# A newly searched order of operations, with sixteen small operations on another engine, in a fused attention and MLP block on one core

## The chip, the cores and the metric

The kernel runs on one NeuronCore of one Trainium2 chip. The metric is the device time of one execution in microseconds (us), taken as the median of several runs. An engine is named as the profile names it: PE is the matmul engine (PEld its weight loads), DVE the vector engine, ACT the scalar engine, POOL the GpSimd engine, and SP the engine whose queue issues all DMA transfers of this kernel.

## What is computed

One transformer-like block on a sequence of 2048 rows of 448 numbers in bf16: a sliding, dilated attention of 16 heads over 8 earlier positions, then a mixer and an MLP, each behind a layer norm.

```python
def _A_ref(x, wqkv, wo):                      # H = 16, W = 8, dilation 2
    q, k, v = split(x @ wqkv)                 # x: (1, 2048, 448)
    logits = einsum(q, k at positions s - 2*w) * scale     # w = 0..7, masked below 0
    return (softmax(logits) @ v at the same positions) @ wo

def _B_ref(x, w1, w2, w3, w4):
    h = gelu(layernorm(x) @ w1)               # 448 -> 448
    hs = (the four quarters of h moved by +1, -1, +2, -2 rows) @ w2
    x1 = x + hs
    return x1 + gelu(layernorm(x1) @ w3) @ w4 # 448 -> 1792 -> 448

h = x + _A_ref(layernorm(x), A_wqkv, A_wo)
out = h + _B_ref(layernorm(h), B_w1, B_w2, B_w3, B_w4)
```

## The kernel before, in words

The sequence is cut into four stretches of 512 rows (t = 0 to 3) for the attention and the mixer, and into five units of 2, 4, 4, 4 and 2 row tiles of 128 (u = 0 to 4) for the MLP. The phase functions only write down operations, each with an engine, its instructions and what it reads and writes; the tag of an operation is the phase and the number of the stretch or unit, so "B20" is phase B2 of unit 0.

- N1 (line 680): statistics of the rows on DVE, the reciprocal root as an Ln and an Exp on ACT, and the normalisation, mostly on DVE.
- A1 (line 696): the transposed rows times the query and key weights; a half of the stretches are transposed by a DMA (`dma_turn`, line 425, "DMA_TRANSPOSE actT<-lntm" in the profile). V (line 743): the values, evicted to vt and moved to vw by DMAs.
- A2 (line 764): four large products of queries and shifted keys on DVE (tile qk_r, 128x4096), each summed over the head by matmuls on PE (ps<-qk_r,zc); then the softmax under the tag S on DVE and ACT.
- A3 (line 814): four products of the attention with a mask on DVE (tile bd_r), the matmuls with vw, and under the tag O the output matmul with wo and the residual.
- B1 (line 860): layer norm and, under the tag M, the matmul with w1 and the gelu on ACT.
- B2 (line 915): the matmul with w2, the sum with the residual on DVE, and under the tag T the layer norm and its transposing DMA; for unit 0 the statistics are sums of squares on ACT. W3 (line 962): the matmul with w3 and the gelu on ACT. B3 (line 979): the matmul with w4, the last sum on DVE and the store.

Operations are numbered from 0 to 872 as they are written down, and the numbers are the same in both kernels. `arrange` (line 197) takes the list ORDER: it goes through it, gives every operation its place in the queue of its engine, and hands out the buffers (8 PSUM banks, 2 of qk_r, 3 of bd_r and so on), first freed first used. Every engine then works through its own queue in that order and waits at each operation on the semaphores of what it needs. An operation that waits holds up all behind it in its queue. OTHER lists the operations that run on their second engine: evictions and normalisations written for ACT then run on DVE, and the additions `xb + xin` of line 957 written for POOL run on DVE. All instructions are issued by one line, so the profile shows nearly every instruction as L1048; a load of ACT's function table shows as L1043 where `emit_engine` sets it ahead of an Exp or Ln that follows a gelu:

```python
            for op in order[e]:
                if op.table == "exp" and table != "exp":
                    eng.preload_act_table_set("natural_log_exp_and_others")
                table = op.table or table
                for (sem, val) in plan_[op.idx]:
                    eng.wait_ge(sem, val)
```

The operations that are spoken of below by number:

- 103: the eviction of the second transposed tile at the start (A10). 196, 198: two normalisations of B10. 510, 513: two evictions of A33.
- 488, 490, 492, 494: the four DVE products of A23 (the queries and keys of stretch 3); 489, 491, 493, 495: the matmuls that sum them (8, 8, 8 and 4 instructions). 497, 501, 502: DVE and PE of its softmax.
- 555: the second pair of matmuls of B20. 557, 556: B20's two residual sums on DVE; 558: minus the mean (nm, DVE); 559, 560: the sums of squares (ACT); 561, 562: Ln and Exp (ACT); 563: nmr (DVE); 564, 565: the two normalisations of T0; 568: the transposing DMA of T0; 577: the first matmul of W30; 579: the first eviction of W30 in the new order (gelu). 310: an Ln of B11.
- 605, 606, 613, 614: the four groups of matmuls of B21, 8 instructions each. 597: the first matmul of B30.
- 300, 308, 309, 313 to 316: last aggregate, Ln, Exp and the four normalisations of B11; 317: its transposing DMA. 481: an eviction of V3.
- 37, 38: the loads of w3, 896 KB each; 486, 487: the loads of w4, 784 KB each; 483, 484, 485: the moves of V3's values to vw (256, 320 and 48 KB).
- 566, 567, 627, 629, 698 to 701, 769 to 771, 830: additions `xb + xin` of the units T0 to T4.

Of the kernel before, what the change touches and what calls it, by code (L numbers as in the profile page):

```python
# [21 lines left out]
STAGE = '....'  # L22
ALONE = False
ORDER = """
# [30 lines left out]
"""  # L55
OTHER = """
103 196 198 510 513 564 565 627 629 699 700 701 769 830
"""
FULL = (4,)
FILL = (1, 1, 0, 0)  # L60
# [1029 lines left out]
```

## Time and profile before

| | us |
|---|---|
| median of 3 runs | 189.72 (188.6, 189.72, 190.02) |
| span of the profiled execution, first to last instruction | 187.0 |
| its own time beside the span | not recorded; the median is 2.7 above the span |
| ACT busy | 124.0 (66% of the span) |
| POOL busy | 20.9 (11%) |
| ACT_TABLE_LOAD | 12 of 1.28 each |
| granted TensorE clock, mean | 1.000 |

The times of the runs hold what lies around the span, so a difference worked out in the span is added to the median. The trace gives each instruction's start and duration; matmuls overlap, so the interval from one start to the next tells what one costs.

### The profile page before, as it was taken

The page shows a single profiled execution, that of the slowest core. Times are in us where ns is not written, and L with a number is a line of the kernel's source. Part 1 is how long each engine was busy: PE and PEld are TensorE (multiplying, and loading weights), DVE is VectorE, ACT ScalarE, POOL GpSimd, SP SyncE. Part 2 cuts the span into 40 slices and gives each one's busy share as a digit, 9 for nine tenths or more (in the row PEclk, how much of TensorE's full clock was granted, in tenths as well). Part 3 has the DMA queues.
Part 4 walks back from the last instruction along what each step waited for, and adds up shares of the span by engine and source line. Part 5 has one row for each costly group of instructions (what it writes and reads, how often), then busy time and mean ns, then how long its engine had stood idle before and what let it go on. Part 6 is the DMA issues. An engine that isn't in the chain of part 4 may idle for free.

```text
span 187.0 us, 5742 instructions
## 1 busy us (share of the span) xinstructions
PE 180.0 (96%) x2482; PEld 93.5 (50%) x2482; DVE 130.8 (70%) x236; ACT 124.0 (66%) x280; POOL 20.9 (11%) x56
## 2 busy tenths in 40 slices
PE   5999999989999989999999999999999999999994
PEld 2685443345453445467455444555444544555663
DVE  7989999999999999999997960089962080000512
ACT  4459989879999999998991987930267004930340
POOL 3440000000003000500042000020034050000000
PEclk9999999999999999999999999999999999999999
DMA  5923583661654697597409060043305031000022
GB/s 151 340 101 58 125 173 63 141 149 17 115 124 94 160 206 301 100 316 146 101 4 140 2 137 4 0 31 84 100 4 112 4 71 60 4 0 0 4 98 74
DMA packets 38609, 18.29 MB, mean 98 GB/s; under 512 B 27464, under 2 KB 38072, under 8 KB 38584
## 3 DMA queue, kind: packets, MB, share of 16 engines
q1 hardware_dynamic: 38584, 17.93, 41.4%
q8 instruction: 19, 0.31, 0.7%
q14 instruction: 6, 0.05, 0.1%
HBM read 8.14 MB, written 1.84 MB: 53 GB/s over the span
## 4 chain that ended last, share of the span: by engine, by line
PE 75%; DVE 16%; ACT 6%; issue 1%; POOL 0%; POOLq 0%
PE ps L1048 75%; DVE bd_r L1048 6%; DVE qk_r L1048 4%; DVE lntm L1048 2%; ACT lntm L1048 1%; DVE xin L1048 1%; DVE st L1048 1%; ACT arena L1048 1%; DVE mx L1048 1%; ACT h3T L1048 1%; ACT L1048 1%; ACT L1043 1%; DVE arena L1048 1%; ACT xin L1048 1%; DVE pb L1048 0%
## 5 line engine op out<-in xcount | busy, mean ns | idle before, releaser
L1048 PE MATMUL ps<-actT,arena 64*128 64x512 bf16 (+2 forms) x812 | 69.6, 326 | 0.3
L1048 ACT ACTIVATE h3T<-ps 128x512 bf16<-128x512 f32 (+1 forms) x70 | 30.7, 520 | 39.1 <-PE ps L1048 38.7
L1048 PEld LDWEIGHTS ps<-actT,arena 64*128 64x128 bf16 (+1 forms) x812 | 35.7, 96 | 29.8 <-PE ps L1048 1.6
L1048 PE MATMUL ps<-arena,h3T 64*128 64x448 bf16 (+3 forms) x434 | 44.5, 343 | 0.0
L1048 DVE SCALAR_TENSOR_TENSOR ost<-ps,mrs,arena 128x448 bf16<-128x448 f32 (+2 forms) x17 | 10.7, 649 | 35.5 <-PE ps L1048 26.9
L1048 ACT ACTIVATE arena<-ps 128x512 bf16<-128x512 f32 (+4 forms) x62 | 31.5, 568 | 2.6 <-PE ps L1048 2.4
L1048 DVE TENSOR_TENSOR qk_r<-arena 128x4096 bf16<-128x4096 bf16 (+1 forms) x16 | 32.1, 2015 | 0.3 <-PE ps L1048 0.3
L1048 PEld LDWEIGHTS ps<-arena,h3T 64*128 64x128 bf16 (+1 forms) x434 | 22.4, 94 | 19.6 <-ACT h3T L1048 0.3
L1048 DVE TENSOR_TENSOR bd_r<-arena,bmask 80x2048 bf16<-80x2048 bf16 x16 | 18.9, 1211 | 0.3 <-ACT arena L1048 0.3
L1048 DVE TENSOR_SCALAR lntm<-arena,mv,rs_y 128x512 bf16<-128x512 f32 x14 | 6.8, 540 | 13.1 <-ACT rs_y L1048 11.6
L1048 POOL TENSOR_TENSOR arena<-arena,xin 128x448 f32<-128x448 f32 x9 | 10.6, 1193 | 34.3 <-DVE lntm L1048 34.3
L1048 PE MATMUL ps<-wo_s,actT 64*128 64x448 bf16 x128 | 14.3, 350 | 0.1
L1048 PE MATMUL ps<-w_s,arena 64*128 64x448 bf16 x88 | 13.3, 350 | 0.0
L1048 PE MATMUL ps<-actT,w_s 64*128 64x512 bf16 (+1 forms) x112 | 13.3, 376 | 0.0
L1048 ACT ACTIVATE lntm<-xin,nm 128x448 bf16<-128x448 bf16 x16 | 10.5, 660 | 4.0 <-DVE nm L1048 4.0
L1048 ACT ACTIVATE actT<-ps 128x512 bf16<-128x512 f32 (+2 forms) x19 | 11.8, 639 | 2.0 <-PE ps L1048 1.9
L1048 PE MATMUL ps<-arena,actT 64*128 64x448 bf16 x112 | 12.6, 350 | 0.1
L1048 DVE SCALAR_TENSOR_TENSOR arena<-xin,rs_y,ps 128x448 f32<-128x448 bf16 x16 | 10.3, 673 | 0.3 <-PE ps L1048 0.3
L1048 DVE BATCH_NORM_STATS2 st<-xin 128x6 f32<-128x448 bf16 x16 | 9.1, 612 | 0.5 <-DMA xin<-in_A_x_dram 0.4
L1048 ACT ACTIVATE vt<-ps 128x448 bf16<-128x448 f32 x16 | 8.4, 543 | 1.0 <-PE ps L1048 1.0
L1048 PEld LDWEIGHTS ps<-wo_s,actT 64*128 64x128 bf16 x128 | 5.9, 94 | 6.1 <-PE ps L1048 0.9
L1048 PEld LDWEIGHTS ps<-actT,w_s 64*128 64x128 bf16 (+1 forms) x112 | 6.0, 98 | 5.6 <-ACT h3T L1048 0.2
(75 smaller groups left out, 167.1 us busy)
## 6 DMA issues: line engine op xcount, KB each, us to landing
arena<-in_B_w_dram SPq DMA_DIRECT2D x2, 896.0 KB, 7.0
out_dram<-ost SPq DMA_DIRECT2D x15, 112.0 KB, 1.8
arena<-in_B_w_dram SPq DMA_DIRECT2D x2, 784.0 KB, 5.8
vw<-vt SPq DMA_DIRECT2D x4, 320.0 KB, 4.1
vw<-vt SPq DMA_DIRECT2D x4, 256.0 KB, 3.5
arena<-in_A_wqkv_dram SPq DMA_DIRECT2D x2, 448.0 KB, 4.5
xin<-in_A_x_dram SPq DMA_DIRECT2D x2, 448.0 KB, 5.1
xin<-in_A_x_dram SPq DMA_DIRECT2D x3, 224.0 KB, 5.3
```

The costliest lines, as they stand in the source:

```text
L1043: eng.preload_act_table_set("natural_log_exp_and_others")
L1048: inst = getattr(eng, meth)(**kw)
```

## The change

ORDER is another permutation of the same 873 operations, and OTHER another list. No instruction is added or left out; an operation that changes its engine takes that engine's form. Eviction 103, normalisation 196, evictions 510 and 513 and normalisations 564 and 565 go from DVE to ACT. Additions 627, 629, 700, 769 and 830 go from DVE to POOL, and 566, 567, 698, 770 and 771 from POOL to DVE. On PE the warm-up matmuls (51 to 59) and the order of the phases stay much as they were; on ACT the gelus and the Exp and Ln stand in fewer, longer stretches.

```diff
--- before.py
+++ after.py
 ORDER = """
-41 42 0 4 1 7 44 45 46 8 43 6 60 61 9 65 66 2 62 63 64 11 10 72 70 73 71 67 68 69 5 74 75 77 96 98 84 51 52 53 54 55
-56 57 58 59 99 101 102 104 107 76 12 13 78 85 105 100 103 115 121 106 108 109 116 110 117 118 122 111 112 123 124 94
...
-308 309 387 316 315 313 314 388 477 194 390 476 400 389 391 394 24 25 26 473 27 371 28 29 359 200 39 201 205 97 202
-204 206 208 203 401 392 207 393 395 396 458 30 36 31 32 33 34 35 554 397 398 399 555 403 310 472 317 318 404 490 557
-556 558 402 322 560 559 561 562 311 407 319 321 320 488 563 565 564 405 408 410 409 567 566 323 325 324 489 491 605
-606 406 411 414 492 494 610 40 37 38 568 485 487 482 486 577 573 578 415 413 412 580 579 574 576 575 493 495 613 569
-614 581 496 497 195 607 416 417 421 423 422 424 425 615 498 570 571 572 593 582 594 618 499 500 611 501 595 583 596
-584 585 589 586 587 590 588 591 592 597 502 504 418 503 598 432 426 433 436 619 616 608 511 427 484 514 483 515 512
...
+0 1 51 52 53 54 55 7 5 45 41 56 57 58 59 42 46 44 8 48 6 2 43 60 61 62 49 63 9 65 66 64 67 10 72 70 68 73 71 74 75 69
+99 101 100 102 103 77 86 104 107 108 12 13 78 84 97 76 90 105 106 79 115 14 209 211 94 15 215 213 216 212 47 214 210
...
+380 477 305 303 381 198 382 479 294 196 32 306 301 480 293 299 302 304 383 359 193 300 371 369 481 308 372 309 384 194
+33 34 313 315 472 460 461 316 456 464 465 476 385 386 462 457 463 314 466 387 388 370 490 200 458 317 390 400 389 394
+201 205 202 203 467 204 459 206 208 207 401 322 318 35 473 323 325 37 554 485 487 402 324 319 321 320 555 395 396 391
+392 397 393 398 483 488 399 489 403 557 556 558 407 492 560 404 406 408 559 561 562 38 405 605 563 484 310 564 491 606
+410 409 411 565 311 414 494 413 607 412 415 493 495 496 497 416 498 610 613 614 615 417 422 423 568 424 421 577 499
+573 578 579 585 574 580 586 576 587 569 575 581 588 570 571 582 500 4 501 584 572 618 486 589 583 502 611 612 504 511
+503 590 514 608 593 505 597 591 609 482 594 596 592 512 425 432 426 595 433 508 513 616 617 619 434 427 307 428 567
...
 OTHER = """
-103 196 198 510 513 564 565 627 629 699 700 701 769 830
+198 566 567 698 699 701 770 771
 """
```

42 rows, old and new, of the table ORDER are left out of this document.

## The prediction, made before the changed kernel ran

> **What bounds the kernel now.** I read the page first, then the busy time by stretches, then the waits of single engines, and last the instructions in order of time around one place. The page's first part:
>
> ```profile
> PE 180.0 (96%) x2482; PEld 93.5 (50%) x2482; DVE 130.8 (70%) x236; ACT 124.0 (66%) x280; POOL 20.9 (11%) x56
> ```
>
> PE is busy in 180.0 of 187.0 us. All of its matmuls stay, so a new order can only win what PE loses now. Where PE loses it, the stretches show (busy time of each engine; the cuts are the arrival of the second x tiles, operation 558 and operation 577):
>
> ```profile
> 8.52:71.48 62.96, 60.79 (x1125) 30.47 (x1123) 61.24 (x86) 56.66 (x136) 4.20 (x22) 1.00 0.57 127
> 71.48:78.70 7.22, 7.16 (x80) 3.35 (x77) 7.15 (x15) 6.92 (x18) 2.61 (x3) 1.00 0.61 176
> 78.70:187.00 108.30, 105.59 (x1258) 56.34 (x1254) 55.59 (x118) 57.00 (x120) 11.25 (x13) 1.00 0.30 65
> ```
>
> The columns are the length, then PE, PEld, DVE, ACT and POOL, then clock, DMA share and GB/s. Up to 71.48 DVE is busy in 61.24 of 62.96 us, as fully as PE: there the two engines run neck and neck, and PE's idle time is time in which it waits for DVE. After 78.70 DVE and ACT are half idle and PE works alone. So the time is set by how soon DVE lets PE enter the long W3 and B3 part, and by how much PE work is then left. DVE's own waits from 8.52 to 71.48 (us in total, times, longest) are few:
>
> ```profile
> DVE lntm L1048 <- ACT rs_y L1048: 0.6, 1, 0.6
> DVE nm L1048 <- ACT lntm L1048: 0.4, 1, 0.4
> DVE st L1048 <- DMA xin<-in_A_x_dram: 0.4, 1, 0.4
> DVE bd_r L1048 <- ACT arena L1048: 0.3, 1, 0.3
> DVE qk_r L1048 <- PE ps L1048: 0.3, 1, 0.3
> ```
>
> **The place I follow.** The entry into W3 is a chain: 558 (nm, DVE), 559 and 560 (squares, ACT), 561 and 562 (Ln, Exp), 563 (nmr, DVE), 564 and 565 (normalise), 568 (transposing DMA), 577 (first matmul of W30). In order of time, each column start, length:
>
> ```profile
> 69.76 1.28 ACT L1043 ACT_TABLE_LOAD   x1
> 71.05 0.30 ACT L1048 ACTIVATE rs_x<-mv,epsilon 128x4 f32<-128x4 f32 x1
> ...
> 71.73 0.66 ACT L1048 ACTIVATE lntm<-arena,nm 128x448 bf16<-128x448 f32 x1
> ...
> 72.39 0.66 ACT L1048 ACTIVATE lntm<-arena,nm 128x448 bf16<-128x448 f32 x1
> ...
> 73.17 0.29 ACT L1048 ACTIVATE rs_x<-mv,epsilon 128x2 f32<-128x2 f32 x1
> 73.49 0.30 ACT L1048 ACTIVATE rs_y<-rs_x 128x2 f32<-128x2 f32 x2
> ```
>
> ```profile
> 71.48 0.17 DVE L1048 TENSOR_SCALAR nm<-mv 128x2 f32<-128x2 f32 x1
> ...
> 73.76 0.15 DVE L1048 TENSOR_TENSOR nmr<-nm,rs_y 128x2 f32<-128x2 f32 x1
> ...
> 73.95 1.00 DVE L1048 TENSOR_SCALAR lntm<-arena,nm,rs_y 128x512 bf16<-128x512 f32 x2
> ...
> 74.98 1.24 SPq L1048 DMA_TRANSPOSE actT<-lntm  x1
> ...
> 77.88 0.09 PEld L1048 LDWEIGHTS ps<-w_a,arena 64*128 64x128 bf16 x1 [0.50 <-PE ps L1048]
> ...
> 78.65 0.82 PE L1048 MATMUL ps<-actT,arena 64*128 64x256 bf16 x12
> ```
>
> From 558 to 577 it takes 78.65 - 71.48 = 7.17 us. The transposing DMA lands 3.1 us after its issue (this view, of the one DMA in that stretch):
>
> ```profile
> DMA to landing us min/median/max: 3.1/3.1/3.1
> ```
>
> That is 78.08, so PE comes to 577 0.57 later: now the chain doesn't quite decide.
>
> **The change part by part, made against the span of 187.0.** The lengths come from these groups (count, busy us and mean ns of one):
>
> ```profile
> L1048 DVE TENSOR_TENSOR qk_r<-arena 128x4096 bf16<-128x4096 bf16 x12 | 27.4, 2281 | 0.3 <-PE ps L1048 0.3
> ...
> L1048 DVE TENSOR_SCALAR lntm<-xin,nm,rs_y 128x512 bf16<-128x512 bf16 x14 | 4.9, 408 | 0.0
> ...
> L1048 PE MATMUL ps<-qk_r,zc 128*32 128x512 bf16 x112 | 7.9, 383 | 0.0
> ...
> L1048 ACT ACTIVATE lntm<-xin,nmr,rs_y 128x512 bf16<-128x512 bf16 x2 | 1.6, 808 | 0.0
> ```
>
> *Start.* POOL builds the identity first, so the warm-up matmuls begin somewhat sooner, and eviction 103 leaves DVE. Both come to nothing: DVE waits 0.4 us for the x tiles (the row of the DMA above), their loads stand at the same place in SP's queue, and from there on DVE sets the pace. If that cover were gone, 103 would give back its 0.4 us.
>
> *DVE ahead of 558.* I compared the two queues of DVE up to 558. They hold the same operations but for three: 103 (above), 196, which goes to ACT (0.41 less), and 488, a product of A23 that now stands ahead (2.28 more). So 558 comes **1.87 us later** by work. Eviction 510 and 513 and the additions lie behind 558, where DVE has room, and are not on the path.
>
> *DVE's waits.* The 0.6 stays: in both orders the first normalisation of N11 directly follows its aggregates, with the Ln and Exp between. The other three (0.4, 0.3, 0.3) may go, since the squares of N13, the first bd_r products and the qk_r products now stand further from what they need: -1.0. New ones appear: the normalisations of B11 now follow their last aggregate 300 with one softmax step (0.6 to 0.7) in between, while ACT does an eviction (481), an Ln and an Exp, about 1.1 us; and 557 follows close on matmul 555, which stands behind M1 and so behind the transposing DMA 317. I put 0.65 on the two. Together **-0.35**; bounds -1.0 (none new) and +0.65 (none goes).
>
> *The chain.* In the new queue of ACT the gelus of M0 and M1 (203 to 208, 320 to 325) stand ahead of 560, and 561 is the first Ln behind them. So a table load of 1.28 stands between 559 and 561, where now it was done at 69.76, ahead of the chain. Next to it 310 (0.30) stands between 562 and 564, beside 563. And 564 and 565 go to ACT, 0.8 each instead of 0.5. From 558: squares and gap 1.69, load 1.28, Ln and Exp 0.6, 563 or 310 0.25, two normalisations 1.55, DMA 3.1 with 0.15 on either side of it: 8.6, that is **+1.43** against 7.17. Bounds: +0.9 (310 and the steps overlap better) to +2.7 (the DMA takes the 4.4 that is the median of all eleven in the page, instead of 3.1). PE can't get past: 577 and all behind it wait in its queue, and B30 and the stores behind W30.
>
> [...]
>
> *The ACT table loads in all.* Going through ACT's queue I count 8 switches between gelu and Exp or Ln instead of 12: 4 x 1.28 = 5.1 less, against some 4 us of evictions and normalisations added (four of 0.5 to 0.6, one of 0.8, the two above). ACT has no less to do that matters, and it isn't what bounds.
>
> *PE ahead of 577.* The queue of PE now holds four more groups ahead of 577: 493 and 495 (12 instructions; 7.9 / 112 each, 0.85) and 613 and 614 (0.77 each: the second group of that kind starts at 77.88 and the next at 78.65). So **2.4 us less** is left behind 577.
>
> *Waits behind 577.* From 78.70 on PE's weight loads now wait (us, times, longest):
>
> ```profile
> PEld ps L1048 <- ACT h3T L1048: 1.3, 5, 0.4
> PEld ps L1048 <- DVE arena L1048: 0.5, 1, 0.5
> ...
> PEld ps L1048 <- DMA vw<-vt: 0.4, 1, 0.4
> ...
> PEld ps L1048 <- DMA actT<-lntm: 0.4, 1, 0.4
> PEld ps L1048 <- DVE lntm L1048: 0.4, 1, 0.4
> PEld ps L1048 <- DVE qk_r L1048: 0.3, 1, 0.3
> ```
>
> Those on qk_r (0.3) and on B21's sum (0.5) belong to 495, 613 and the sums that free their banks, now ahead of 577, where PE waits for the chain anyway. W30's first evictions now follow a gelu load and four squares, which may cost some tenths. I take **-0.5**; bounds -1.6 and +0.6.
>
> *Sum:* 1.87 - 0.35 + 1.43 - 2.4 - 0.5 = **+0.05**. The stall moves from many small waits into one ahead of W30, and the total is unchanged: span 187.0, and 189.72 + 0.05 = **189.8** for the median. With all lower bounds it is -2.2, with all upper ones +3.4.
>
> **The rivals.**
>
> *The waits go and nothing comes in their place.* DVE loses 1.0 with no new wait, and behind 577 the waits on DVE and DMA (0.5 + 0.4 + 0.4 + 0.4 + 0.3 = 2.0) go: 1.87 - 1.0 + 1.43 - 2.4 - 2.0 = -2.1, **187.6**. For it speaks that many weights are asked for earlier in SP's queue; against it that DVE is 97% busy up to 558, and that the table load of the chain is fixed by the order.
>
> *Slower: the weights stand in the way of the transposing DMA.* SP now issues 37, 487 and 38 and the three moves 485, 483 and 484 between 317 and 568: 896 + 784 + 896 + 624 = 3200 KB, all by one queue, where before 568 only 37 and 38 had gone.
>
> ```profile
> 64.18 2.33 SPq L1048 DMA_TRANSPOSE actT<-lntm  x1
> 66.56 1.50 SPq L1048 DMA_DIRECT2D arena<-in_B_w_dram  x2
> ```
>
> ```profile
> arena<-in_B_w_dram SPq DMA_DIRECT2D x2, 896.0 KB, 7.0
> ...
> arena<-in_B_w_dram SPq DMA_DIRECT2D x2, 784.0 KB, 5.8
> ```
>
> The first two rows are 317 and the loads 37 and 38 behind it, the last two KB and us to landing. With 196 and a softmax step (387) now behind it, 317 goes out about 1 us sooner, takes 2.3, and the weights start near 65.5; 568 is ready at 558 + 5.4 = about 78.4, that is 12.9 later. The two loads of w3 now bring 1.8 MB in about 8 us with their start, some 250 to 300 GB/s by their landing; then 3.3 MB take 11 to 13 and are through at 76.5 to 78.6, just in time. At the 176 GB/s of the stretch from 71.48 they need 18.6, until 84, and 568 lands over 5 later. It decides from about 255 GB/s downwards. Half of the worst is my price, +2.5: **192.3**. Load 486 stands behind 568 as well; landing 5.8 later, it meets 597, which is some 5 us of PE behind 577, with little to spare.
>
> *The clock.* At the start warm-up matmuls keep PE busy; starting sooner while the x tiles don't, PE idles some tenths between transposes. The trace grants 1.00 in all stretches from 8.52 on. If PE came to the first products at half rate, A10's 6 us of matmuls would take up to 3 longer, half of it hidden behind DVE: +1.5, **191.3**. [...]
>
> **How the numbers follow.** A measurement of this kernel can tell about 1% from no change, 1.9 us: below 187.8 is faster, above 191.6 slower. The forecast has 0.67 (faster 0.03, same 0.60, slower 0.04), the first rival 0.16 (0.11, 0.05, 0), the weights 0.12 (0, 0.04, 0.08), the clock 0.05 (0, 0.03, 0.02). That gives faster 0.14, same 0.72, slower 0.14. The forecast's own range is 188.1 to 191.6; the range to hold 8 in 10 reaches out to the first rival and most of the way to the second: 187.6 to 192.0.
>
> **What would show it.** In the changed profile: 8 table loads, one of them between the squares and the Ln of T0; nm of T0 at about 73.0 with a 4096-wide product more ahead of it; the transposing DMA issued near 78.4, W30's first matmul near 81.6 and PE idle for a us or more before it; DVE waits of 0.6 at N11 and about 0.4 at B11. The forecast is wrong if W30 starts before 80.5 or after 83, if PE's waits behind it sum to well under a us or over 3, or if the first products after the start run at half the rate of before.

## The result, and the profile after

The changed kernel takes **191.38 us** in the median (191.18 to 191.74, 4 runs), the kernel before 189.75 (188.6 to 190.02, 4 runs): a ratio of **1.0107**, 95% interval [1.0061, 1.0152]. The forecast was 189.8. The result lies inside the predicted range (187.6 to 192.0), 1.6 us above its middle, and on the edge of the 1% within which I had called two times the same. The profiled execution took 191.47 with a span of 189.8; what lies around the span is 1.7. By that, before's profiled execution (span 187.0) took about 188.7, one of the quick ones, so the spans differ by more (2.8) than the medians (1.63). Runs that took over 1.5% longer than the fastest of their kernel are left out of the ratios below (two of the four with 63 pairs, one of the four with 488 behind 558, one of the ten with the small load), and the profiled executions with 63 pairs and with 488 behind 558 are such.

The page of the changed kernel:

```profile
PE 180.4 (95%) x2482; PEld 93.1 (49%) x2482; DVE 130.2 (69%) x230; ACT 122.9 (65%) x282; POOL 20.2 (11%) x56
...
PE 54%; DVE 28%; DMA 9%; ACT 6%; issue 1%; POOL 1%; DVEq 0%; POOLq 0%
...
L1047 PE MATMUL ps<-actT,arena 64*128 64x512 bf16 (+2 forms) x812 | 69.9, 326 | 2.2 <-DMA actT<-lntm 2.0
...
L1047 PE MATMUL ps<-actT,w_s 64*128 64x512 bf16 (+1 forms) x112 | 13.2, 376 | 1.5 <-DMA actT<-lntm 1.5
```

PE's work is the same; PE idles longer, and what it idles for are transposing DMAs: 2.0 ahead of matmuls of W3 (568 and 631) and 1.5 ahead of M1 (317). The three stretches of the prediction, cut here at the first matmul of the projections, 558 and 577 (length, then PE, PEld, DVE, ACT, POOL, clock, DMA share, GB/s):

```profile
8.67:73.63 64.96, 62.74 (x1145) 31.91 (x1143) 62.92 (x87) 56.63 (x138) 4.60 (x22) 1.00 0.61 140
73.63:83.81 10.18, 8.34 (x90) 3.25 (x86) 9.80 (x21) 10.03 (x25) 0.00 (x0) 1.00 0.79 165
83.81:189.80 105.99, 102.95 (x1228) 55.38 (x1228) 50.34 (x108) 51.92 (x111) 12.44 (x15) 1.00 0.24 51
```

Against the prediction's rows: start +0.15, up to 558 +2.00, from 558 to 577 **+2.96**, behind 577 **-2.31**; together +2.80, the whole difference of the spans. The first cut isn't quite the same: 8.52 was the arrival of the second x tiles, and the first matmul of the projections came at 8.40, so that up to 558 it is +1.88 and the start is +0.27; the third cut (78.70, with 577 at 78.65) moves 0.05 more. PE's loss in them (length less busy) was 2.17, 0.06 and 2.71 and is now 2.22, 1.84 and 3.04.

The entry into W3 in order of time (start, length; in brackets the idle time ahead and what ended it):

```profile
72.30 0.68 DVE L1047 SCALAR_TENSOR_TENSOR arena<-xin,rs_y,ps 128x448 f32<-128x448 bf16 x1 [1.36 <-PE ps L1047]
...
73.63 0.17 DVE L1047 TENSOR_SCALAR nm<-mv 128x2 f32<-128x2 f32 x1
...
74.14 0.68 ACT L1047 ACTIVATE lntm<-arena,nm 128x448 bf16<-128x448 f32 x1
...
75.57 1.28 ACT L1042 ACT_TABLE_LOAD   x1
76.87 0.29 ACT L1047 ACTIVATE rs_x<-mv,epsilon 128x2 f32<-128x2 f32 x1
...
77.43 0.16 DVE L1047 TENSOR_TENSOR nmr<-nm,rs_y 128x2 f32<-128x2 f32 x1
...
77.63 1.52 ACT L1047 ACTIVATE lntm<-arena,nmr,rs_y 128x512 bf16<-128x512 f32 x2
...
79.17 1.27 SPq L1047 DMA_TRANSPOSE actT<-lntm  x1
...
83.80 0.72 PE L1047 MATMUL ps<-actT,arena 64*128 64x256 bf16 x10 [1.37 <-DMA actT<-lntm]
```

From 558 to the issue of 568 it takes 5.54; the forecast had 5.4, with the table load where it was expected. From the issue to 577 it takes 4.64, and there the forecast had 3.2 to 3.25. The landings of 568 and of 317, one view each, and the DMA engines while 568 is under way:

```profile
DMA to landing us min/median/max: 4.6/4.6/4.6
```

```profile
DMA to landing us min/median/max: 6.0/6.0/6.0
```

```profile
DMA  0000000000000699999999998959990000072000
...
q8 instruction: 1, 0.02, 1.4%
```

Before, they landed in 3.1 and 4.7. The first row of the last view is the busy share of the DMA engines from 79.15 to 83.00, in tenths, in 40 slices. It is zero for the 1.2 us behind the issue: the bulk loads ahead of 568 in SP's queue were through. Then 568 moves for about 1.5 us, and among its packets is one that no operation of the kernel asked for: one transfer of 16 KB on the queue that the profile calls *instruction*.

**What I took from that.** The trace of the changed kernel has 19 such 16 KB transfers. Behind 128 us one comes about every 251 instructions of PE (a matmul and its weight load are two), and over the whole trace one every 255 in the mean with PE's semaphore instructions counted, so I read them as blocks of PE's own code, fetched while it runs. Three of them come at 65.40, 81.26 and 103.83, inside the stretches of 317, 568 and 631, the three transposing DMAs that land late (6.0, 4.6, 6.1). Two more transposing DMAs of four tiles (issued at 44.03 and 124.12) have a block 4 us behind their issue as 317 and 631 have, and land in 4.8 and 4.3, so that a block there doesn't always make a landing late. So the theory is: the stall ahead of W30 is there because 568 lands late, and it lands late because a **block of code** is fetched in its stretch. The rivals: the load 486 (784 KB) that follows 568 at once; the engines of the moved operations; DVE's extra product 488; the table load.

### The profile page after: what moved, and what is told of

It reads as the page before. It is cut to its first block, busy times and chain, and to the rows that moved or that the text cites. A ratio compares the mean times of both kernels' runs of the same rounds, so it can differ in the third digit from the quotient of the medians.

```text
span 189.8 us, 5741 instructions
## 1 busy us (share of the span) xinstructions
PE 180.4 (95%) x2482; PEld 93.1 (49%) x2482; DVE 130.2 (69%) x230; ACT 122.9 (65%) x282; POOL 20.2 (11%) x56
## 3 DMA queue, kind: packets, MB, share of 16 engines
HBM read 8.14 MB, written 1.84 MB: 53 GB/s over the span
## 4 chain that ended last, share of the span: by engine, by line
PE 54%; DVE 28%; DMA 9%; ACT 6%; issue 1%; POOL 1%; DVEq 0%; POOLq 0%
PE ps L1047 54%; DVE qk_r L1047 11%; DMA actT<-lntm 9%; DVE bd_r L1047 5%; DVE lntm L1047 4%; DVE st L1047 3%; ACT lntm L1047 2%; DVE mx L1047 1%; ACT arena L1047 1%; DVE pb L1047 1%; ACT actT L1047 1%; ACT vt L1047 1%; DVE ls L1047 1%; DVE mv L1047 1%; DVE xin L1047 1%
## 5 line engine op out<-in xcount | busy, mean ns | idle before, releaser
L1047 ACT ACTIVATE h3T<-ps 128x512 bf16<-128x512 f32 (+1 forms) x70 | 31.6, 516 | 43.5 <-PE ps L1047 43.1
L1047 DVE TENSOR_SCALAR lntm<-arena,mv,rs_y 128x512 bf16<-128x512 f32 x14 | 7.3, 568 | 12.8 <-ACT rs_y L1047 9.9
L1047 ACT ACTIVATE actT<-ps 128x512 bf16<-128x512 f32 (+2 forms) x22 | 13.0, 644 | 1.8 <-PE ps L1047 1.7
L1047 PE MATMUL ps<-wo_s,actT 64*128 64x448 bf16 x128 | 13.8, 350 | 0.2 <-ACT actT L1047 0.2
L1047 POOL TENSOR_TENSOR arena<-arena,xin 128x448 f32<-128x448 f32 x9 | 9.1, 1030 | 14.7 <-DVE lntm L1047 12.7
L1047 POOL TENSOR_TENSOR rs_y<-rs_x,mhalf 128x4 f32<-128x4 f32 (+1 forms) x3 | 3.1, 1047 | 69.1 <-DVE rs_x L1047 63.6
L1047 PE MATMUL ps<-qk_r,zc 128*32 128x512 bf16 x112 | 8.8, 384 | 0.5 <-DVE qk_r L1047 0.5
```

The source lines that it names most:

```text
L1047: inst = getattr(eng, meth)(**kw)
```

## Is it the code or the load behind? (four runs)

The blocks can be moved without touching the order: more instructions ahead of everything bring each of them earlier in the program.

```diff
         def warm():
             for n in range(WARM):
-                keep_busy()
+                b = _Tile(P_bank)
+                mms([(b(lambda v, j=j: v[:, j * 128:(j + 1) * 128]), ident[:], ident[:, 0:128], True, True, 128, None)
+                     for j in range(4)])
```

That is the run with 27 more pairs; those with 63 and 99 have 8 pieces of 64 and 12 of 42 columns.

*27 pairs.* 

> The changed kernel with each of the 9 warm-up matmuls (512 columns) cut into 4 of 128 columns: 27 more pairs of weight load and matmul in PE's queue ahead of everything, same columns, same order. Theory (blocks): in the changed kernel the landings of 317 (6.0 instead of 4.5), 568 (4.6 instead of 3.1) and 631 (6.1 instead of 4.3) are late because a 16 KB transfer of the instruction queue falls into each of their stretches (65.40, 81.26, 103.83); these come every 256 PE instructions, so 54 more instructions ahead bring the one of 81.26 to about 78.4, before the first packet of 568. Then 568 lands in 3.1 to 3.3, W30's first matmul comes 1.4 sooner after 558 (8.8 instead of 10.2), span 188.4 or less; 317 may still be hit. Rival (load behind): 568 is late because load 486 (784 KB) follows it at once; nothing changes, landing 4.6, span 189.8. Rival (DVE and ACT work alone): neither.

*63 pairs.* 

> As the run with 27 more pairs, but each warm-up matmul is cut into 8 of 64 columns: 63 more pairs, 126 PE instructions. Theory (blocks): the block of 81.26 comes at some 76 to 77, the one of 65.40 at 58 to 60, inside the transposing DMA 200 (57.5 to 62) instead of 317; 317 lands in 4.5, 568 in 3.1; 558 up to 1.3 sooner, chain 558 to 577 8.8; span 187.0 to 188.4. Rival (load behind): 568 lands in 4.6, span 189.5 to 190.

*99 pairs.* 

> As before, each warm-up matmul cut into 12 of 42 columns: 99 more pairs, 198 PE instructions. Theory (blocks): no block falls into 200, 317, 568 or 631 (by the counts of PE instructions they come near 57, 69, 75, 86, 97 and 105): 317 lands in 4.5, 568 in 3.1, 631 in 4.3; 558 up to 1.3 sooner, 8.8 from 558 to 577, PE's wait at 631 (1.0) gone: span 186.0 to 187.5. Rival (load behind): 568 lands in 4.6, span 189.5 to 190.

*A small load behind 568* (six of the seven chunks of that half of w4 are left out):

```diff
-                dma("w4%d" % f, w4_s[:, f:f + 7, :], w4_v[:, f:f + 7, :], 128 * 7 * D * 2).odeps.add(last)
+                m = 7 if f else 1
+                dma("w4%d" % f, w4_s[:, f:f + m, :], w4_v[:, f:f + m, :], 128 * m * D * 2).odeps.add(last)
```

> The changed kernel with load 486 cut from 784 KB to 112 KB (one of its seven chunks; the other six chunks of that half of w4 are left out), at the same place in SP's queue right behind 568. Rival (load behind): without the bulk behind it 568 lands in 3.1, chain 558 to 577 8.7, span 188.3. Theory (blocks): the 16 KB transfer stays in 568's stretch, the landing stays at 4.3 to 4.7 and the span at 189.4 to 189.9.

Measured. With the small load 568 still lands late (first view below), with a block among its packets, and the stretch from 558 to 577 keeps its 10.08. With 99 pairs the landing is 3.5 (second view). The stretch is 9.02 with 27 pairs and 9.03 with 99:

```profile
DMA to landing us min/median/max: 4.5/4.5/4.5
```

```profile
DMA to landing us min/median/max: 3.5/3.5/3.5
```

```profile
74.38:84.46 10.08, 8.33 (x88) 3.25 (x86) 9.70 (x20) 9.93 (x25) 0.00 (x0) 1.00 0.72 154
```

```profile
74.63:83.65 9.02, 8.10 (x89) 3.27 (x87) 8.27 (x17) 8.61 (x23) 0.00 (x0) 1.00 0.78 192
```

```profile
73.92:82.95 9.03, 8.12 (x86) 3.16 (x86) 8.68 (x18) 8.90 (x24) 0.00 (x0) 1.00 0.89 205
```

So the load behind falls and the block stands. With 27 pairs the trace gives no landing of 568; the block goes at 80.10, just ahead of the issue at 80.17, and 577 comes 3.47 after the issue instead of 4.64. There 317 still has a block 1.9 behind its issue and lands in 5.4. With 99 pairs 317 and 631 land in 4.3 and 4.4 too, as expected (and the one at 139, which landed in 4.8 in the changed kernel, now has a block 3.9 behind its issue and lands in 6.0). But the whole gains little: ratios 1.0086 [1.0059, 1.0113] with 27 pairs, 1.0069 [1.0045, 1.0092] with 99, 1.0074 [1.0037, 1.0110] with the small load. None can be told from the 1.0107 of the unchanged order, and the spans that I had expected (186.0 to 188.4) came out at 189.1 and 189.0. Where the rest went is asked below.

With 63 pairs something else happened: four runs of 191.47 to 195.04 us, a ratio of 1.0169 [1.0079, 1.0260]. In the profiled execution 317 and 568 land in 4.3 and 3.2, as the theory has it, but PE stood still in the middle of a group of eight matmuls that have all their data:

```profile
72.47 0.61 PE L1049 MATMUL ps<-qk_r,zc 128*32 128x512 bf16 x6
76.19 0.61 PE L1049 MATMUL ps<-qk_r,zc 128*32 128x512 bf16 x2 [3.12 <-issue]
```

*Issue* means that PE waited for nothing that the profile shows. PE had issued 480 instructions since the block before (fetched at 60.4), and the next one went at 73.5, amid the bulk loads, when PE had stood for 0.4 us. In no other trace does PE issue more than 446 from one block to the next. The stop is seen in this one execution; that PE had run out of code is read from it, not tried.

## Engines, product 488, and the work ahead of W30 (four runs)

*The engines alone*, in the order of before:

```diff
 OTHER = """
-103 196 198 510 513 564 565 627 629 699 700 701 769 830
+198 566 567 698 699 701 770 771
```

> The kernel before with its own ORDER and the changed kernel's OTHER: only the engines change (103, 196, 510, 513, 564, 565 to ACT; 627, 629, 700, 769, 830 to POOL; 566, 567, 698, 770, 771 to DVE). Theory (the order lengthens the entry into W3): the two normalisations of T0 on ACT put 0.5 to 0.6 on the chain from 558 to 577, of which PE's lateness of 0.57 there hides most; span within 0.5 of 187.0, time within 0.4% of before. Rival (engines): the slowdown of about 1% comes from these operations on ACT and POOL; ratio near 1.01.

Measured: 1.0140 [1.0110, 1.0170]. The expectation of at most 0.4% failed, and the number is the rival's: the engines alone, in the old order, cost at least as much as the whole change. The view of ACT shows why: a normalisation that moves to ACT takes its place in ACT's queue, and in the old order that is behind a table load and two gelus.

```profile
75.08 0.30 ACT L1048 ACTIVATE rs_y<-rs_x 128x2 f32<-128x2 f32 x2
75.39 1.28 ACT L1048 ACT_TABLE_LOAD   x1
76.69 1.09 ACT L1048 ACTIVATE arena<-ps 128x512 bf16<-128x512 f32 x2
77.66 1.51 ACT L1048 ACTIVATE lntm<-arena,nmr,rs_y 128x512 bf16<-128x512 f32 x2
```

568 is issued 6.16 after 558 instead of 3.50, and 577 comes after 9.28 instead of 7.17. I had priced the move at 0.5 by the durations and left out the queue. In its own order the change pays 0.8 each for the two and no such wait; so I don't take this for the cause in the changed kernel; there the two normalisations were moved back only together with other operations (below). It agrees with the entry into W3 setting the time.

*488 behind 558*:

```diff
-... 398 483 488 399 489 403 557 556 558 407 492 560 404 406 408 559 561 562 38 405 605 563 484 ...
+... 398 483 399 403 557 556 558 488 407 560 404 406 408 489 559 561 562 38 405 605 563 492 484 ...
```

> The changed kernel with product 488 (2.28 on DVE) moved behind 558, its matmul 489 behind 408 on PE and product 492 behind 563, as the product's buffer asks. By the forecast's step (488 ahead of 558 makes 558 late): 558 comes up to 2.28 sooner, at 71.4. By the trace of the changed kernel: DVE waits 1.44 for matmul 555 right ahead of 557 although 488 stands ahead of it, and 555 stands behind M1 on PE, which waits for the landing of 317; so 558 stays at 73.4 to 73.9, DVE's wait there grows to some 3.7, and the products that are now late put 0.5 to 2 on the span (190.3 to 191.8).

Measured: DVE has 2.28 less to do ahead of 558, and 558 doesn't come sooner; DVE waits longer for matmul 555 (the stretch up to 558, and DVE's only wait in the last 14 us of it):

```profile
8.33:74.32 65.99, 62.58 (x1137) 31.74 (x1135) 60.97 (x86) 56.64 (x138) 6.43 (x27) 1.00 0.62 142
```

```profile
DVE arena L1047 <- PE ps L1047: 3.7, 1, 3.7
```

The other executions of the new order with 317 late need as much for this stretch (65.75 to 65.99, the profiled one 64.96). Behind 558 the late products make 577 come 12.22 after it, in a stretch with a granted clock of 0.89. The time is 1.0178 [1.0122, 1.0235], about what was expected (190.3 to 191.8): three runs have spans of 190.0 to 191.9. With 99 pairs, where 317 lands in 4.3, DVE doesn't wait there at all, and the stretch still takes 65.54: then 488 fills it. So I read two paths of about one length that end at 558: taking away either one gained nothing in these traces, and no run takes away both.

*The matmuls that were moved ahead, moved back*:

```diff
-... 412 415 493 495 496 497 416 498 610 613 614 615 417 422 423 568 424 421 577 499 573 578 ...
+... 412 415 416 610 417 422 423 568 424 421 577 573 578 493 495 496 497 498 613 614 615 499 ...
```

> The changed kernel with the matmuls 493, 495, 613 and 614 (2.4 us on PE) moved back behind 577, 573 and 578, with the operations that depend on them. Theory (568 decides when W30 starts, and work moved ahead of it only fills the wait): 577 stays where it is after 558 (10.0 to 10.4), PE's wait ahead of it grows from 1.8 to about 4, and the part behind grows by 2.0 to 2.5: span 191.8 to 192.3. Rival (PE's work ahead is itself the bound): 577 comes up to 2.4 sooner and the span stays at 189.5 to 190.

Measured: 577 comes 10.47 after 558, so with 568 landing as late as here (4.9) PE's work ahead of it is no bound, as the theory has it. But the time grows far more, to 1.0393 [1.0342, 1.0445]: PE's wait ahead of 577 is now 5.3 us, and over the 5.38 us behind it the granted clock is 0.68 (its longest wait, and two stretches behind it; the last three columns: granted clock, DMA share, GB/s):

```profile
PEld ps L1047 <- DMA actT<-lntm: 5.3, 1, 5.3
```

```profile
84.62:90.00 5.38, 5.32 (x50) 2.53 (x52) 1.38 (x2) 0.13 (x1) 0.00 (x0) 0.68 0.86 199
90.00:95.00 5.00, 4.07 (x84) 3.19 (x80) 3.83 (x7) 4.77 (x13) 0.00 (x0) 1.00 0.00 0
```

In the first row the granted clock is 0.50 from 84.65 to 88.05 and 1.00 behind it, which gives the 0.68. Shorter waits went with a lower clock too: behind one of 2.4 (with 488 behind 558) it is 0.50 from 83.77 to 87.17, which gives the 0.89 of the stretch from 558 to 577 there, and at the stop of 3.1 with 63 pairs it is 0.50 from 75.37 to 82.19, with 0.76 in the mean of that kernel's 14.47 us from 558 to 577. The waits of up to 1.9 us that are shown for the other kernels left it at 1.00.

*The table load put on the chain of the kernel before*:

```diff
-... 555 403 310 472 317 318 404 490 557 556 558 402 322 560 559 561 562 311 ...
+... 555 403 472 317 318 404 490 557 556 558 402 322 560 559 561 562 310 311 ...
```

> The kernel before with 310, the Ln that has ACT load the table at 69.76, moved behind 562: the load of 1.28 then falls between the squares (559) and the Ln of T0 (561), as in the changed kernel. Theory: the chain from 558 to 568's issue grows by 1.28 from 3.50 to 4.8; PE, which came 0.57 after the landing, now waits for it, so that 577 comes 0.7 later after 558 (7.9) and the span grows by 0.5 to 0.8 (0.3 to 0.4%). Rival (the entry into W3 decides nothing): 577 and the span stay within 0.2.

Measured: 1.0066 [1.0045, 1.0086], 1.25 us for a load of 1.28. 568 is issued 4.72 after 558 and lands in 3.1, but 577 comes after 8.69, not 7.9 (ACT in order of time, then PE's waits in the stretch):

```profile
73.75 1.28 ACT L1042 ACT_TABLE_LOAD   x1
...
76.01 1.28 ACT L1047 ACT_TABLE_LOAD   x1
77.31 2.06 ACT L1047 ACTIVATE arena<-ps 128x512 bf16<-128x512 f32 x4
```

```profile
PEld ps L1047 <- DVE xin L1047: 1.9, 1, 1.9
PEld ps L1047 <- PE ps L1047: 0.5, 1, 0.5
PEld ps L1047 <- ACT arena L1047: 0.4, 1, 0.4
```

PE waits for neither 568 nor the load itself. The additions of O2, whose banks the matmuls need, stand behind 563 to 565 in DVE's queue, and the gelus of M1 behind the load and one more in ACT's; both are now later, and when the landing is there (79.91), PE is still at 606. One load delayed three things that PE needs.

## Taking the stall away (four runs)

*No table switch ahead of W30* (the gelu of two of the four mixer stretches is left out):

```diff
-                    act(gT[0:m, g, at:at + 512], b(lambda v: v[0:m, :]), ACT.Gelu_apprx_tanh)
+                    act(gT[0:m, g, at:at + 512], b(lambda v: v[0:m, :]), ACT.Copy if t < 2 else ACT.Gelu_apprx_tanh)
```

> The changed kernel with the four gelus of M0 and the four of M1 replaced by plain copies of the same size on ACT (this leaves the gelu of two of the four mixer stretches out): ACT's table then stays at Exp and Ln, and the load of 1.28 between the squares of T0 and its Ln is gone, as is the one ahead of M0. Theory (the load lies on the chain into W3): 568 is issued 4.2 to 4.4 after 558 instead of 5.5, and its packets pass before the 16 KB block of PE's code comes (81.3), so it lands in 3.1 to 3.6; 577 then comes when PE has done the work ahead of it, 8.6 to 8.9 after 558 instead of 10.2; time 1.2 to 1.5 less than the changed kernel, ratio 1.003 to 1.005. Rival (PE's own work or DVE sets 577): 577 stays at 10.0 or more after 558, ratio 1.008 to 1.011.

This is where my theory of the chain fell. ACT is done with Ln and Exp 1.3 sooner, and then waits for DVE (of ACT and of DVE):

```profile
76.42 0.20 ACT L1047 ACTIVATE rs_y<-rs_x 128x2 f32<-128x2 f32 x1
...
78.11 1.52 ACT L1047 ACTIVATE lntm<-arena,nmr,rs_y 128x512 bf16<-128x512 f32 x2 [1.29 <-DVE nmr L1047]
```

```profile
74.23 2.29 DVE L1047 TENSOR_TENSOR qk_r<-arena 128x4096 bf16<-128x4096 bf16 x1
76.82 0.62 DVE L1047 SCALAR_TENSOR_TENSOR xin<-ps,xin 128x448 bf16<-128x448 f32 x1 [0.30 <-PE ps L1047]
...
77.92 0.15 DVE L1047 TENSOR_TENSOR nmr<-nm,rs_y 128x2 f32<-128x2 f32 x1
```

563 stands in DVE's queue behind product 492 and two additions, and comes 3.79 after 558 with the load gone as it did with the load (77.43 - 73.63 = 3.80). 568 is issued 5.52 after 558 instead of 5.54. 577 does come after 8.80, and what is shorter is the part behind the issue (3.28 instead of 4.64): the block of code went at 77.9 this time, ahead of 568's packets. The trace gives no landing here. So 577 came when expected, but not by the shorter chain that was to bring it. The profiled execution is at 190.23 us, but the ten runs reach from 190.2 to 192.81 with a median of 191.62, ratio 1.0112 [1.0076, 1.0148]. So a sooner 577 doesn't show in the median here.

*564 and 565 on DVE, and 613 and 614 ahead of 495; and both that and 99 pairs*:

```diff
-... 405 605 563 484 310 564 491 606 410 409 411 565 311 414 494 413 607 412 415 493 495 496 497 416 498 610 613 614 615 417 ...
+... 405 605 563 564 565 484 310 491 606 410 409 411 311 414 494 413 607 412 415 493 416 417 610 613 614 495 496 497 498 615 ...
-198 566 567 698 699 701 770 771
+198 564 565 566 567 698 699 701 770 771
```

> The changed kernel with the normalisations 564 and 565 back on DVE, right behind 563, and on PE 613 and 614 ahead of 495 (with the operations that hang on 495 behind it), so that PE has work while DVE is late with 494. Theory: 568 is issued 0.5 to 0.6 sooner after 558 (5.0); the landing keeps most of its lateness (3.5 to 4.6, the 16 KB block comes at the end of its packets), 577 9.0 to 9.8 after 558, ratio 1.005 to 1.010. Rival (the engine of two normalisations is what makes the changed kernel slow): ratio 1.000 to 1.003.

> Both edits together: 564 and 565 on DVE with 613 and 614 ahead of 495, and each warm-up matmul cut into 12 pieces (99 more pairs in PE's queue). Theory: 317, 568 and 631 land without a block in their stretch (4.3 to 4.5, 3.1 to 3.5, 4.4), 568 is issued 5.0 after 558, and 577 comes 8.3 to 8.6 after 558, when PE's work ahead of it is done; ratio 1.003 to 1.006, against 1.007 with the cut warm-up alone. It does not beat the kernel before, because 558 itself comes 1.5 to 2 later there.

Measured: the entry is even shorter than expected, 8.69 and 8.12 from 558 to 577, and PE idles only 0.28 and 0.08 in it. The time is no better and misses both expectations: 1.0135 [1.0084, 1.0185] and 1.0140 [1.0100, 1.0180]. PE gives it back behind 577, where it loses 4.25 and 4.64 (length less busy up to the end), against 3.04 in the changed kernel (waits of the weight loads from 577 on; first the kernel with both edits, then the one without a table switch for comparison):

```profile
PEld ps L1049 <- ACT h3T L1049: 2.8, 3, 1.4
PEld ps L1049 <- DVE ls L1049: 0.7, 1, 0.7
```

```profile
PEld ps L1047 <- ACT h3T L1047: 0.7, 2, 0.5
```

W30's own evictions are gelus behind the squares, the Ln and the Exp of B12 and S3 in ACT's queue. When W30 starts sooner, its PSUM banks can wait for ACT. But a sooner start alone doesn't bring so long a wait: where 577 comes 8.80 to 9.03 after 558 with the Exp of S3 in its old place, these waits are 0.2 (27 pairs), 0.7 (no table switch) and 1.1 (99 pairs). My own edit set that Exp later, and how much of the 2.8 is its doing wasn't tried.

*The control: the kernel before with 99 pairs.* 

> The kernel before with each warm-up matmul cut into 12 pieces (99 more pairs): the control of that edit. If cutting the warm-up costs something by itself, it shows here as 0.3% or more with all landings as they were. Theory (blocks): which transposing DMAs land late changes with where the 16 KB transfers fall; if one falls into the stretch from 1.2 to 2.6 us after the issue of 568, that one lands in 3.5 to 4.6 instead of 3.1 and 577 comes up to 1 later; 631 (5.5 in the kernel before, with a block in it) lands in 4.3 to 4.5 if none does. Ratio 0.997 to 1.005.

Measured: 188.57 us against 189.48 beside it, ratio **0.9954** [0.9932, 0.9977], 10 and 19 runs: cutting the warm-up costs nothing, the time is a little under the range that I had expected, and this version beats both kernels. In its trace 568 lands in 3.1 and 631 in 4.6 (5.5 before), and PE's wait of 0.4 on 631 is gone; 317 lands in 5.7, but there the matmuls 554, 555 and 403 stand ahead of M1 and PE doesn't wait for it. The 0.4 is half of the 0.9; where the other half comes from isn't settled, since its profiled execution was the slowest of its ten.

This control says one thing more. The same cut gained the new order as much: 1.0069 against the 1.0107 without it. With 99 pairs in both, the new order is slower by 1.0069 / 0.9954 = 1.012 (1.008 to 1.015, if the two intervals are taken as independent), no less than without. So the late landings stand in the trace, but nothing shows that they set the two orders apart in time. The stretches of the two kernels with 99 pairs show what is left (the old order, then the new one's first and last; its middle one is the 9.03 above):

```profile
8.19:72.31 64.12, 60.98 (x1127) 30.61 (x1127) 62.27 (x87) 56.91 (x136) 4.82 (x25) 1.00 0.60 128
72.31:79.42 7.11, 7.05 (x77) 3.31 (x75) 7.04 (x15) 6.78 (x16) 2.60 (x3) 1.00 0.57 164
79.42:187.60 108.18, 105.60 (x1258) 59.08 (x1254) 55.71 (x118) 57.03 (x121) 11.25 (x13) 1.00 0.27 66
```

```profile
8.38:73.92 65.54, 63.23 (x1144) 31.46 (x1143) 63.55 (x87) 56.91 (x139) 6.07 (x27) 1.00 0.63 136
82.95:189.00 106.05, 103.00 (x1228) 58.51 (x1228) 51.41 (x110) 52.90 (x112) 12.44 (x15) 1.00 0.23 53
```

Up to 558 it is +1.42, from there to 577 +1.92, behind it -2.13, with 568 landing in 3.1 and 3.5. The part from 558 to the issue of 568 alone is 2.00 longer (3.50 and 5.50). That is one execution of each.

## Why the prediction was right, and where it was not

The time was right because terms of 1.5 to 3 us with opposite signs cancel in good part. That it stayed in the range is partly luck: the chain came out +3.0, beyond its upper bound of +2.7, with a landing of 4.6 beyond the 4.4 that I had allowed and for a reason that I hadn't thought of, and the other terms left room for it. One execution of each order isn't enough to size them, since the first stretch varies from one to the next: from the first matmul of the projections to 558 it takes 63.1 to 64.9 in four of the old order (64.0 in the mean) and 65.0 to 66.2 in eight of the new one (65.6). By these the change costs about 1.6 there, some 3.0 from 558 to 577 where 568 lands late, and it saves about 2.5 behind. That is 2.1, against 1.63 measured in the medians and 0.05 forecast.

- *Start:* right. No wait and no clock below 1.00 behind it; the rival of the clock falls. No run shows its half rate at the start, nor the 3 us that it would cost: from the first matmul of the projections to 558 the granted clock is 1.00 in every kernel, and a lower one (0.50) is seen only around the waits of 2.4 to 5.3 us told above.
- *DVE ahead of 558 (+1.87 - 0.35 = +1.52; 73.0 forecast, 73.63 measured):* right in size, and its cause only half. 488 is there, but with 488 taken away 558 stayed. What I called a small new wait (0.25 of the 0.65) is 1.4: matmul 555 behind M1, behind 317, which took 6.0 instead of 4.7. The 0.4 that I expected at B11 isn't there, nor are the four small waits; only the 0.6 stayed.
- *The chain (+1.43; 8.6 forecast, 10.18 measured):* the mis-sized term. The part up to 568's issue was right in number (5.4 and 5.54) and wrong in mechanism: the table load isn't alone on it, since 492 and two additions hold 563 just as long. The terms as written also add up to 8.8 and not 8.6 (5.37, then 3.1 with 0.15 on either side). The landing was 4.6 where I took 3.1 and bounded it by 4.4. These 1.5 are about as much as the forecast was too low, but that doesn't make them the cause: with 568 landing in 3.5 the stretch was 1.15 shorter and the time at most 0.4%, and the same edit gained the old order as much. Without the lateness the chain is still +1.9 in place of +1.43.
- *The weights ahead of 568 (the slower rival):* falls. From 67.3 to 76.9 the DMA engines moved 312 GB/s, and they were idle when 568 was issued, so 568 was late for another reason. My rate for it was a slip: 1.8 MB in 8 us are 225 GB/s, not 250 to 300, and by that the weights would have come through only near 80, behind the 78.4 that I had for 568.
- *PE ahead of 577 (-2.4) and the waits behind (-0.5):* -2.31 measured instead of -2.9. Most of the small waits of before are gone, as forecast, but one of 1.0 is new: 631, with a block in its stretch, lands in 6.1 instead of 5.5.
- *The first rival (the waits go):* falls; PE's loss grew from 4.9 to 7.1.
- *The table loads:* 8 instead of 12, as counted, and ACT's busy time fell by 1.1, as 5.1 less against some 4 more has it. What that is worth wasn't tried.

By the prediction's own marks the forecast failed in one: W30 was to start between 80.5 and 83, and started at 83.8. A second is on its edge: PE's waits behind it were to stay under 3, and PE loses 3.0 there.

What stays open: no single edit brought the new order back to the time of before. With those three landings free of blocks it keeps 0.7% [0.45, 0.92] against the kernel before and 1.2% against that kernel with the same cut, and with the entry short as well PE loses the same behind it. So the later 558 and the longer chain up to 568's issue, less what is saved behind 577, are what the traces leave for the cause; no run takes both away. PE's busy time in the three stretches is 173.6 to 174.2 in the old order and 174.0 to 174.9 in the new, with the same matmuls and a clock of 1.00; why wasn't tried.

## What to carry to other kernels

In an order that a search has balanced, several paths end at the same place at the same time: 555 and 488 at 558, the table load and 492 at 563, the landing, PE's work and ACT's evictions around 577. A step's price then is what lies on it beyond the next path, and that has to be looked up in every engine's queue, not only along the chain that one follows. And an operation that changes its engine costs its place in the new queue before it costs its duration: with the engines alone 568 was issued 2.66 later after 558 (6.16 instead of 3.50), where the durations said 0.5.

## What the runs showed of the hardware

*A 16 KB transfer beside a transposing DMA.* Over the traces of all fourteen kernels (one profiled execution each; landings that the trace gives), a transposing DMA of four tiles without a 16 KB block within 4.6 us of its issue lands in 4.3 to 5.0 us (63 cases, median 4.4), one of two tiles in 3.1 to 3.5 (17 cases). With a block that starts 1.9 to 2.9 us after the issue, four tiles took 5.2 to 5.7 (8 cases); with one at 1.9 to 2.1 two tiles took 4.5 to 4.9 (4), with one at 2.7 only 3.1 and 3.3. With one at 0.4 to 1.3 us four tiles took 4.5 to 5.7 (15 cases), and there the issue itself took 2.8 to 3.3 us. With one at 3.8 to 4.1 us four tiles took either 4.3 to 4.8 (18 cases) or 5.9 to 6.1 (13); what decides between the two isn't known. For 568, the edits that left the block among its packets kept the lateness, and 99 pairs, which moved it away, took it away. That these transfers are PE's code is my reading of the queue's name and of the count (about 251 instructions of PE from one to the next). The longest time that PE's weight loads waited for nothing that the profile shows is 3.6 us in the trace with the one stop above, and 0.5 to 1.0 us in those of the kernel before, of the changed one and of those with 27 pairs, 99 pairs and the small load.

*A long PE wait cost twice.* Behind 5.3 us of waiting (493, 495, 613 and 614 moved back) the matmuls ran at a mean granted clock of 0.68 for the next 5.4 us, and behind 2.4 us (488 behind 558) at 0.50 from 83.77 to 87.17; behind the 1.8 us ahead of 577 in the changed kernel at 1.00.
